# A gated linear recurrence and its two-layer MLP on one core: v cast on GpSimd, merged masks and state sums, other PSUM banks, another order of the weight loads

## The chip, the cores and the metric

One core of a Trainium2 chip runs the whole program. The metric is the device time of one execution in microseconds. Engines are named as in the profile: PE (TensorE matmul), PEld (its weight loads), DVE (VectorE), ACT (ScalarE), POOL (GpSimd), SP (SyncE, which issues every DMA here).

## The reference

Inputs r, k, v, w have the shape (4, 8, 768, 48): batch, head, position, head dimension; u is (8, 48). All are float32, and so is the output, (3072, 384).

```python
for t in range(S):
    cur = np.einsum('bhd,bhe->bhde', u[None] * kt, vt)
    y[:, :, t] = np.einsum('bhd,bhde->bhe', rt, state + cur)
    state = wt[:, :, :, None] * state + np.einsum('bhd,bhe->bhde', kt, vt)
...
h = x @ w_in                     # x: y as (3072, 384); w_in: 384 x 2048
g = np.maximum(0.01 * h, h)
return (g @ w_out)               # w_out: 2048 x 384
```

## The kernel before, in words

**Chunks.** The 768 positions of each of the 4 batches are cut into 6 chunks of 128, 24 chunks in all (NCH), and a chunk carries all 8 heads: its tiles are 128 positions x 384 columns. Within a batch the state goes from chunk to chunk. After the scan of a chunk comes its MLP.

**Scan of a chunk** (loop from line 283). Four loads bring w, k, r, v into one slot of the ring `in` (L297). ACT takes the logarithm of w (L317). PE sums it from the chunk's end with a triangular matrix and adds the totals of four head pairs (cp, L332, L337). DVE adds the logarithm again (ci, L347), ACT takes two exponentials (er L354, ek L360) and a third for the totals (a, L435), and DVE multiplies r and k with them (rk, L367, L373). PE transposes r and k, eight transposes in one step into the bank se (L385); DVE copies the r half out (rkT, L392), ACT the k half (L396). PE makes the scores, even heads in se and odd heads in so (L471); DVE masks each bank (m, two operations, L494). v is cast to bf16 on DVE (vb, L323). PE forms the chunk's sums of k times v (pp, L482). POOL scales the state with the totals, in two halves of 64 partitions (sb, L462); DVE adds pp (s, two halves, L510, or a copy in the first chunk of a batch, L508). PE adds up the output yp from rkT, sb and from m, vb (L522, L526). The u term goes by POOL and DVE: ru (L411, L415), its row sum dg (L419), times v (vs, L423). DVE adds it to yp (y, L537), PE transposes y into the bank so (L547), and ACT copies the result into xT (L553).

**MLP of a chunk.** Four up pieces (each 12 matmuls into one of two banks hp, L579), each followed by ACT's leaky ReLU (g, L613); four down quarters (each 4 matmuls into op, L631); DVE copies op (L642) and SP stores it (L646). The weights come once, four loads of 768 KB for w_in (L250) and four for w_out (L255), through slots of the same ring `in`, and DVE and ACT cast half each (L273, L275).

**What sets the order.** Every operation is a step with an engine, an assumed duration, a priority and its dependencies. The class Plan (line 16) runs a list schedule over them: the free engine takes the ready step of the lowest priority number. Each engine then executes its steps in the order that came out, whatever the real durations are. Scan steps of chunk n have the priority 10n or little more, MLP steps 1000 and up, ACT's g 5, output copies 3. `WEIGHTS` holds for each weight load the chunk ahead of whose loads it is planned, and its priority: w_in ahead of chunk 1 with 4, w_out ahead of chunk 3 with 24. The logarithm of chunk n waits for the first up piece of chunk n-4 (LEAD), the loads of chunk n for the sums cp of chunk n-5 (AHEAD). A ring of one tile makes a step wait until the readers of the tile's last use are done. PSUM has eight banks: hp two, and op, cp, se, so, yp, pp one each.

Of the kernel before, what the change touches and what calls it, by code (L numbers as in the profile page):

```python
# [8 lines left out]
F32 = mybir.dt.float32  # L9
# [6 lines left out]
class Plan:  # L16
# [3 lines left out]
    LAT = 0.12  # L20
# [15 lines left out]
    def order(self):  # L36
# [18 lines left out]
        while events:  # L55
# [14 lines left out]
            if self.wire[i] is None:  # L70
                done[i] = free[e] + self.LAT
            else:
                dma_free = max(dma_free, free[e]) + self.wire[i]
                done[i] = dma_free + 1.7
# [41 lines left out]
def kernel(  # L116
# [11 lines left out]
    nc = tc.nc  # L128
# [11 lines left out]
    APE = 24  # L140
# [4 lines left out]
    WEIGHTS = [(1, 4)] * 4 + [(3, 24)] * 4  # L145
# [22 lines left out]
    er_r = ring("er", 3, [128, H, 64], F32)  # L168
# [8 lines left out]
    a_r = ring("a", 3, [128, NP], F32)  # L177
    sx_r = ring("s", 3, [128, NP, D], F32)
# [5 lines left out]
    dram = ctx.enter_context(tc.tile_pool(name="dram", bufs=1, space=bass.MemoryType.DRAM))  # L184
    ad_r = ring("ad", 4, [1, H * 64], F32, dram)
    hp_r = ring("hp", 2, [128, 512], F32, psum)
    op_r = ring("op", 1, [128, DM], F32, psum)
    cp_r = ring("cp", 1, [128, 512], F32, psum)
    se_r = ring("se", 1, [128, NP, 128], F32, psum)
    so_r = ring("so", 1, [128, NP, 128], F32, psum)  # L190
    yp_r = ring("yp", 1, [128, H, D], F32, psum)
    pp_r = ring("pp", 1, [128, NP, 2, D], F32, psum)

    with tc.manual_schedule():
# [3 lines left out]
        for t in sb_r.tiles:  # L198
            nc.gpsimd.memset(t[:], 0.0)
        for t in er_r.tiles:  # L200
            nc.gpsimd.memset(t[:], 1.0)
# [31 lines left out]
        def dve(n, src=60):  # L233
            return (src + n) / 960.0 + 0.03

        def act(n, src=180):
            return (src + n) / 1200.0
# [7 lines left out]
        def weight_steps(q, which, pri):  # L245
# [16 lines left out]
            for half, eng in ((0, "DVE"), (1, "ACT")):  # L262
# [13 lines left out]
                d = dve(384) if eng == "DVE" else act(768, 224)  # L276
# [6 lines left out]
        for n in range(NCH):  # L283
# [19 lines left out]
            if n == 0:  # L303
# [18 lines left out]
                "DVE", dve(DM // 2),  # L322
                lambda vb=vb, vn=vn: nc.vector.tensor_copy(out=vb.t[:], in_=vn.t),  # L323
# [4 lines left out]

            a_pe = n < APE

            def cum(cp=cp, lw=lw, tot=(not first and a_pe)):
# [3 lines left out]
                if tot:  # L335
# [6 lines left out]
            s_cum = step("PE", 0.35 if not first and a_pe else 0.17, cum, P0, reads=[lw], writes=[cp], deps=[s_ln])  # L342
# [12 lines left out]
                    out=er.t[:, :, 0:D], in_=cp.t[:, 0:DM].rearrange("p (h d) -> p h d", h=H), func=AF.Exp),  # L355
                P0, reads=[cp], writes=[er], deps=[s_cum],
# [9 lines left out]
                "DVE", dve(DM),  # L366
                lambda rk=rk, rn=rn, er=er: nc.vector.tensor_tensor(  # L367
                    out=rk.t[:, 0, :, 0:D], in0=rn.t, in1=er.t[:, :, 0:D], op=ALU.mult),
# [3 lines left out]
                "DVE", dve(DM),  # L372
# [6 lines left out]
            if n < NPE:  # L379
                tr = se_r.take()  # L380
                trv = tr.t[:].bitcast(BF16).rearrange("p a (b t) -> p (a b) t", b=2)

                def tpose(rk=rk, trv=trv):
                    for g in range(2 * NP):
                        nc.tensor.transpose(  # L385
                            trv[:, g, :],
                            rk.t[:, g // NP, 2 * (g % NP) : 2 * (g % NP) + 2, :].rearrange("p h d -> p (h d)"),
                            ident[:])
                s_tr = step("PE", 0.6, tpose, P0, reads=[rk], writes=[tr], deps=[s_r, s_k])
                s_t1 = step(  # L390
                    "DVE", dve(512, 120),
                    lambda trv=trv, rkT=rkT: nc.vector.tensor_copy(out=rkT.t[:, 0:NP, :], in_=trv[:, 0:NP, :]),  # L392
                    P0, reads=[tr], writes=[rkT], deps=[s_tr])
                s_t2 = step(
                    "ACT", act(512),
                    lambda trv=trv, rkT=rkT: nc.scalar.copy(out=rkT.t[:, NP:, :], in_=trv[:, NP:, :]),  # L396
                    P0, reads=[tr], writes=[rkT], deps=[s_tr])
                s_T = [s_t1, s_t2]
            else:
                s_T = [step(  # L400
                    "SP", 0.6,
                    lambda rk=rk, rkT=rkT: nc.sync.dma_start_transpose(
                        out=rkT.t[:], in_=rk.t[:].rearrange("p a h d -> p (a h d)")),
                    P0, reads=[rk], writes=[rkT], deps=[s_r, s_k], wire=1.0)]
# [13 lines left out]
                "DVE", dve(DM),  # L418
# [3 lines left out]
                "POOL", 1.05,  # L422
# [5 lines left out]
            se, so, yp = se_r.take(), so_r.take(), yp_r.take()  # L428
            sb = None
            if not first:  # L430
                a_in = a_r.take()
                if a_pe:
                    s_adep = step(
                        "ACT", act(NP),
                        lambda a_in=a_in, cp=cp: nc.scalar.activation(  # L435
                            out=a_in.t[:], in_=cp.t[:, DM : DM + NP], func=AF.Exp),
                        P0 + 1, reads=[cp], writes=[a_in], deps=[s_cum])
                else:

                    ad = ad_r.take()  # L440
                    s_row = step(
                        "SP", 0.45,
                        lambda ad=ad, er=er: nc.sync.dma_start(
                            out=ad.t[:], in_=er.t[0:1].rearrange("o h d -> o (h d)")),
                        P0 + 1, reads=[er], writes=[ad], deps=[s_er], wire=0.02)
                    s_sp = step(
                        "SP", 0.45,
                        lambda ad=ad, a_in=a_in: nc.sync.dma_start(
                            out=a_in.t[:], in_=ad.t[:].rearrange("o (p q) -> q (o p)", p=NP)),
                        P0 + 1, reads=[ad], writes=[a_in], deps=[s_row], wire=0.4)  # L450
                    s_adep = step(
                        "DVE", dve(NP),
                        lambda a_in=a_in: nc.vector.reciprocal(out=a_in.t[:], in_=a_in.t[:]),
                        P0 + 1, reads=[a_in], deps=[s_sp])
                s_in, s_sdep = prev
                sb = sb_r.take()
                s_sb = []
                for half in range(2):
                    q0 = 64 * half
                    s_sb.append(step(  # L460
                        "POOL", 0.5,
                        lambda sb=sb, s_in=s_in, a_in=a_in, q0=q0, half=half: nc.gpsimd.tensor_tensor(  # L462
                            out=sb.t[q0 : q0 + 64, :, half, :], in0=s_in.t[q0 : q0 + 64],
                            in1=a_in.t[q0 : q0 + 64].unsqueeze(2).to_broadcast([64, NP, D]), op=ALU.mult),
                        P0 + 1, reads=[s_in, a_in], writes=[sb], deps=[*s_sdep, s_adep]))

            def scores(rkT=rkT, se=se, so=so):
                for p in range(NP):
                    for par, sc in enumerate((se, so)):
                        q0 = 64 * par  # L470
                        nc.tensor.matmul(  # L471
                            sc.t[:, p, :], lhsT=rkT.t[q0 : q0 + D, NP + p, :],
                            rhs=rkT.t[q0 : q0 + D, p, :], start=True, stop=True, skip_group_check=True)

            s_sc = step("PE", 0.42, scores, P0 + 1, reads=[rkT], writes=[se, so], deps=s_T)

            if not last:
                pp = pp_r.take()

                def sums(pp=pp, rk=rk, vb=vb):  # L480
                    for p in range(NP):
                        nc.tensor.matmul(  # L482
                            pp.t[:, p, :, :],
                            lhsT=rk.t[:, 1, 2 * p : 2 * p + 2, :].rearrange("p h d -> p (h d)"),
                            rhs=vb.t[:, 2 * p : 2 * p + 2, :],
                            start=True, stop=True, skip_group_check=True)

                s_pp = step("PE", 0.24, sums, P0 + 1, reads=[rk, vb], writes=[pp], deps=[s_k, s_vb])
            m = m_r.take()
            s_m = []  # L490
            for par, sc in enumerate((se, so)):
                s_m.append(step(
                    "DVE", dve(NP * 128, 120),
                    lambda m=m, sc=sc, par=par: nc.vector.tensor_tensor(  # L494
                        out=m.t[:, par, :, :], in0=sc.t[:],
                        in1=maskb[:].unsqueeze(1).to_broadcast([128, NP, 128]), op=ALU.mult),
                    P0 + 1, reads=[sc], writes=[m], deps=[s_sc]))


            if not last:  # L500
                sx = sx_r.take()
                s_st = []
                for half in range(2):
                    def state(half=half, sx=sx, pp=pp, sb=sb):
                        q0 = 64 * half
                        o, i = sx.t[q0 : q0 + 64], pp.t[q0 : q0 + 64, :, half, :]
                        if sb is None:
                            nc.vector.tensor_copy(out=o, in_=i)  # L508
                        else:
                            nc.vector.tensor_tensor(  # L510
                                out=o, in0=i, in1=sb.t[q0 : q0 + 64, :, half, :], op=ALU.add)

                    s_st.append(step(
                        "DVE", dve(NP * D, 120), state, P0 + 1,
                        reads=[pp] + ([] if sb is None else [sb]), writes=[sx],
                        deps=[s_pp] + ([] if sb is None else s_sb)))
                prev = (sx, s_st)

# [166 lines left out]
```

## Time and profile before

| | |
|---|---|
| median of the 2 runs | 222.24 us (221.99 and 222.48) |
| profiled execution | 222.69 us, span in the trace 220.8 us |
| busy, of the span | PE 84%, PEld 65%, DVE 70%, ACT 54%, POOL 45% |
| mean granted TensorE clock | 0.969 |
| DMA | 30.47 MB; 107179 packets, 100368 of them under 512 B |
| from an input load's issue to its landing | 4.1 to 4.4 us median; a weight load 8.2 to 8.7 |

The busy share of an engine counts the time in which it works on at least one instruction. In a table of windows each row is a stretch of the span with the busy microseconds of each engine and, in brackets, the number of its instructions; PEclk is the granted clock, DMA share the mean busy share of the 16 DMA engines. In a row of a group stand the line, engine, operation, output and inputs, then the total busy time, the mean of one in ns, and the idle time just before them with what ended it. In the waits, three figures are the total, the number of times and the longest.

### The profile page before, as it was taken

To read this page: it belongs to the slowest core of one execution; us is meant where nothing else is said; L and a number is where in the kernel's file an instruction comes from. 1 tells how busy PE (TensorE), PEld (TensorE's weight loads), DVE (VectorE), ACT (ScalarE), POOL (GpSimd) and SP (SyncE) were. 2 spreads that over 40 slices of the span, in tenths; PEclk is the share of its full clock that TensorE was granted. 3 is DMA by queue.
4 is the path that set the end of the run, shared out by engine and by line. 5 is a ranking of instruction groups with operands and counts; after the bars stand their busy time and mean duration, and the time that the engine had idled before them with its cause. 6 is when DMAs were issued, how large, how long until landed. Compare 5 with 4: busy or idle time off the path is not lost.

```text
span 220.8 us, 6043 instructions
## 1 busy us (share of the span) xinstructions
PE 186.3 (84%) x2448; PEld 144.2 (65%) x2448; DVE 155.6 (70%) x299; ACT 118.7 (54%) x245; POOL 98.6 (45%) x125
## 2 busy tenths in 40 slices
PE   0446679887979998949899999999999999999983
PEld 0246457665667776736686778777777777788861
DVE  6653995589999999996878876977967565620021
ACT  3347367565566655615465547656555655545420
POOL 6312740687663965666787573474412211200000
PEclk9999559999999999988999999999999999999999
DMA  7999999999999999939089267846010110001101
GB/s 130 318 355 184 297 355 165 179 193 189 200 185 216 188 210 201 200 76 181 18 162 177 61 122 147 174 98 128 36 39 2 37 39 36 3 36 39 39 36 71
DMA packets 107179, 30.47 MB, mean 138 GB/s; under 512 B 100368, under 2 KB 105616, under 8 KB 107152
## 3 DMA queue, kind: packets, MB, share of 16 engines
q1 hardware_dynamic: 107152, 30.09, 64.7%
q8 instruction: 19, 0.31, 0.6%
q14 instruction: 8, 0.07, 0.1%
HBM read 25.36 MB, written 4.72 MB: 136 GB/s over the span
## 4 chain that ended last, share of the span: by engine, by line
PE 49%; DVE 23%; DMA 8%; ACT 7%; issue 7%; SPq 2%; POOL 2%; DVEq 0%; ACTq 0%; POOLq 0%
PE hp L579 19%; PE op L631 18%; DVE rk L373 4%; DVE ci L347 3%; DMA in<-in_moe_w_in_dram 3%; DVE m L494 3%; PE se L385 3%; DVE s L510 3%; PE se L471 3%; DMA in<-in_w_dram 2%; DVE y L537 2%; ACT er L354 2%; DMA in<-in_r_dram 2%; DVE vb L323 2%; PE so L547 2%
## 5 line engine op out<-in xcount | busy, mean ns | idle before, releaser
L579 PE MATMUL hp<-xT,w_in_b 128*128 128x128 bf16 x1152 | 81.0, 225 | 0.8 <-ACT xT L553 0.8
L613 ACT ACTIVATE g<-hp 128x512 bf16<-128x512 f32 x96 | 57.4, 598 | 39.4 <-PE hp L579 38.5
L631 PE MATMUL op<-w_out_b,g 128*128 128x384 bf16 x384 | 77.8, 329 | 0.6 <-DVE o L642 0.6
L579 PEld LDWEIGHTS <-w_in_b 128*128 128x128 bf16 x1152 | 72.5, 101 | 7.5 <-issue 1.2
L631 PEld LDWEIGHTS <-g 128*128 128x128 bf16 x384 | 33.1, 98 | 16.5 <-issue 1.8
L462 POOL TENSOR_TENSOR sb<-s,a 64x192 bf16<-64x192 f32 x40 | 25.6, 639 | 28.8 <-ACT a L435 24.9
L411 POOL TENSOR_TENSOR ru<-in,ub 128x384 f32<-128x384 f32 x24 | 24.7, 1033 | 25.0 <-DMA in<-in_r_dram 21.1
L423 POOL TENSOR_TENSOR vs<-in,dg 128x384 f32<-128x384 f32 x24 | 20.0, 834 | 35.2 <-DVE dg L419 11.4
L642 DVE COPY o<-op 128x384 f32<-128x384 f32 x24 | 13.3, 555 | 23.2 <-PE op L631 22.8
L415 POOL TENSOR_TENSOR ru<-ru,in 128x384 f32<-128x384 f32 x24 | 25.7, 1074 | 1.5
L385 PE MATMUL se<-ident,rk 128*128 128x128 bf16 x192 | 18.3, 230 | 7.8 <-DVE rk L367 3.9
L396 ACT COPY rkT<-se 128x512 bf16<-128x512 bf16 x24 | 14.0, 585 | 19.2 <-DVE rkT L392 12.8
L494 DVE TENSOR_TENSOR m<-se,maskb 128x512 bf16<-128x512 f32 x24 | 16.5, 689 | 6.8 <-ACT g L613 3.7
L385 PEld LDWEIGHTS <-rk 128*128 128x128 bf16 x192 | 12.5, 101 | 12.7 <-DVE rk L373 6.0
L367 DVE TENSOR_TENSOR rk<-in,er 128x384 bf16<-128x384 f32 x24 | 18.2, 759 | 2.3 <-ACT er L354 2.1
L347 DVE TENSOR_TENSOR ci<-cp,lw 128x384 f32<-128x384 f32 x24 | 13.3, 553 | 8.3 <-PE cp L337 5.1
L373 DVE TENSOR_TENSOR rk<-in,ek 128x384 bf16<-128x384 f32 x24 | 18.0, 750 | 1.2 <-ACT ek L360 1.1
L537 DVE TENSOR_TENSOR y<-yp,vs 128x384 bf16<-128x384 f32 x24 | 13.2, 550 | 7.8 <-PE yp L526 7.7
L354 ACT ACTIVATE er<-cp 128x384 f32<-128x384 f32 x24 | 11.8, 491 | 10.6 <-DVE ci L347 6.1
L547 PE MATMUL so<-ident,y 128*128 128x128 bf16 x72 | 8.5, 231 | 9.5 <-DVE y L537 9.2
L494 DVE TENSOR_TENSOR m<-so,maskb 128x512 bf16<-128x512 f32 x24 | 16.3, 680 | 0.0
L360 ACT ACTIVATE ek<-ci 128x384 f32<-128x384 f32 x24 | 12.5, 520 | 5.8 <-DVE ci L347 5.8
(42 smaller groups left out, 193.1 us busy)
## 6 DMA issues: line engine op xcount, KB each, us to landing
in<-in_w_dram SPq DMA_DIRECT2D x24, 192.0 KB, 4.2
in<-in_k_dram SPq DMA_DIRECT2D x24, 192.0 KB, 4.1
in<-in_r_dram SPq DMA_DIRECT2D x24, 192.0 KB, 4.4
in<-in_v_dram SPq DMA_DIRECT2D x24, 192.0 KB, 4.4
out_dram<-o SPq DMA_DIRECT2D x24, 192.0 KB, 2.0
in<-in_moe_w_in_dram SPq DMA_DIRECT2D x4, 768.0 KB, 8.2
in<-in_moe_w_out_dram SPq DMA_DIRECT2D x4, 768.0 KB, 8.7
ub<-in_u_dram SPq DMA_DIRECT2D x1, 192.0 KB, 5.0
```

The source lines that it names most:

```text
L347: lambda cp=cp, ci=ci, lw=lw: nc.vector.tensor_tensor(out=ci.t[:], in0=cp.t[:, 0:DM].rearrange("p (h d) -> p h d", h=H), in1=lw.t[:, :, 0: ...
L367: lambda rk=rk, rn=rn, er=er: nc.vector.tensor_tensor(out=rk.t[:, 0, :, 0:D], in0=rn.t, in1=er.t[:, :, 0:D], op=ALU.mult),
L373: lambda rk=rk, kn=kn, ek=ek: nc.vector.tensor_tensor(out=rk.t[:, 1, :, 0:D], in0=kn.t, in1=ek.t[:], op=ALU.mult),
L385: nc.tensor.transpose(trv[:, g, :], rk.t[:, g // NP, 2 * (g % NP) : 2 * (g % NP) + 2, :].rearrange("p h d -> p (h d)"), ident[:])
L411: lambda ru=ru, rn=rn: nc.gpsimd.tensor_tensor(out=ru.t[:], in0=rn.t, in1=ubv, op=ALU.mult),
L415: lambda ru=ru, kn=kn: nc.gpsimd.tensor_tensor(out=ru.t[:], in0=ru.t[:], in1=kn.t, op=ALU.mult),
L423: lambda vs=vs, vn=vn, dg=dg: nc.gpsimd.tensor_tensor(out=vs.t[:], in0=vn.t, in1=dg.t[:].unsqueeze(2).to_broadcast([128, H, D]), op=ALU.mult),
L462: lambda sb=sb, s_in=s_in, a_in=a_in, q0=q0, half=half: nc.gpsimd.tensor_tensor(out=sb.t[q0 : q0 + 64, :, half, :], in0=s_in.t[q0 : q0 + 6 ...
L494: lambda m=m, sc=sc, par=par: nc.vector.tensor_tensor(out=m.t[:, par, :, :], in0=sc.t[:], in1=maskb[:].unsqueeze(1).to_broadcast([128, NP, ...
L579: nc.tensor.matmul(hp.t[:, a * N : (a + 1) * N], lhsT=w_in_b[:, t, (j + a) * 128 : (j + a + 1) * 128], rhs=xT[:, t, c0 : c0 + N], start=(a ...
L613: lambda hp=hp, g=g, j=j, J=J, N=N: nc.scalar.activation(out=g.t[:, j : j + J, 0:N], in_=hp.t[:, 0 : J * N].rearrange("p (a n) -> p a n", ...
L631: nc.tensor.matmul(op.t[:], lhsT=g.t[:, j, off : off + 128], rhs=w_out_b[:, j, :], start=(j == 0), stop=(j == NJ - 1))
```

## The change

- The v cast goes from DVE to POOL. Both masks are one DVE operation of 1024 columns over a tile `sc` of two banks. The state has both heads of a pair side by side, so sb is one POOL operation and s one DVE operation of 384 columns; the totals' exponential is two ACT operations of 64 partitions each, into a tile that is zero elsewhere.
- The transposes of r and of k are two steps of four, each in its bank of `sc`, each with its copy. The scores use the same tile afterwards.
- pp, yp and the transposes of y share one bank, `yp`. The output op has two banks.
- w_in is requested ahead of chunk 2 with priority 14, w_out ahead of chunk 4 with 34.
- The planner's latencies and many assumed durations are other numbers. A branch that was not used (totals by way of DRAM) is gone.

```diff
-    LAT = 0.12
+    LAT = {"PE": 0.28, "DVE": 0.07, "ACT": 0.07, "POOL": 0.07, "SP": 0.07}
...
-    WEIGHTS = [(1, 4)] * 4 + [(3, 24)] * 4
+    WEIGHTS = [(2, 14)] * 4 + [(4, 34)] * 4
...
-    op_r = ring("op", 1, [128, DM], F32, psum)
+    op_r = ring("op", 2, [128, DM], F32, psum)
     cp_r = ring("cp", 1, [128, 512], F32, psum)
-    se_r = ring("se", 1, [128, NP, 128], F32, psum)
-    so_r = ring("so", 1, [128, NP, 128], F32, psum)
-    yp_r = ring("yp", 1, [128, H, D], F32, psum)
-    pp_r = ring("pp", 1, [128, NP, 2, D], F32, psum)
+    yp_r = pp_r = ring("yp", 1, [128, 512], F32, psum)
+    sc_r = ring("sc", 1, [128, 2, NP, 128], F32, psum)
...
             s_vb = step(
-                "DVE", dve(DM // 2),
-                lambda vb=vb, vn=vn: nc.vector.tensor_copy(out=vb.t[:], in_=vn.t),
+                "POOL", 0.8,
+                lambda vb=vb, vn=vn: nc.gpsimd.tensor_copy(out=vb.t[:], in_=vn.t),
                 P0 + 2, reads=[vn], writes=[vb], deps=[vl],
...
+                for a, s_d, eng in ((0, s_r, "DVE"), (1, s_k, "ACT")):
+                    def tpose(rk=rk, trv=trv, a=a):
+                        for g in range(NP):
+                            nc.tensor.transpose(
+                                trv[:, a, g, :],
+                                rk.t[:, a, 2 * g : 2 * g + 2, :].rearrange("p h d -> p (h d)"),
+                                ident[:])
...
+                    s_tr = step("PE", 0.23, tpose, P0, reads=[rk], writes=[tr], deps=[s_d])
...
+                for half in range(2):
+                    q0 = 64 * half
+                    s_adep.append(step(
+                        "ACT", 0.17,
+                        lambda a_in=a_in, cp=cp, q0=q0, half=half: nc.scalar.activation(
+                            out=a_in.t[q0 : q0 + 64, :, half], in_=cp.t[q0 : q0 + 64, DM : DM + NP], func=AF.Exp),
...
+                s_sb = [step(
+                    "POOL", 1.05,
+                    lambda sb=sb, s_in=s_in, a_in=a_in: nc.gpsimd.tensor_tensor(
+                        out=sb.t[:].rearrange("p g a d -> p (g a) d"),
+                        in0=s_in.t[:].rearrange("p g a d -> p (g a) d"),
+                        in1=a_in.t[:].rearrange("p g a -> p (g a)").unsqueeze(2).to_broadcast([128, H, D]),
...
+            s_m = [step(
+                "DVE", 1.2,
+                lambda m=m, sc=sc: nc.vector.tensor_tensor(
+                    out=m.t[:].rearrange("p a g t -> p (a g) t"),
+                    in0=sc.t[:].rearrange("p a g t -> p (a g) t"),
+                    in1=maskb[:].unsqueeze(1).to_broadcast([128, H, 128]), op=ALU.mult),
...
+                        nc.vector.tensor_tensor(out=sx.t[:], in0=pp.t[:, 0:DM].rearrange("p (g a d) -> p g a d", g=NP, a=2), in1=sb.t[:], op=ALU.add)
...
-                tr = so_r.take()
-                trv = tr.t[:].bitcast(BF16).rearrange("p a (b t) -> p (a b) t", b=2)
+                trv = yp.t[:].bitcast(BF16).rearrange("p (g t) -> p g t", t=128)
```

The change moves instructions on every engine. On SP, at the start, before (in_69 holds chunk 0, in_70 to in_73 w_in, in_74 chunk 1):

```order
L306 DMA ub<-in_u_dram 128x384
L250 DMA in_70<-in_moe_w_in_dram 128x3x512
L250 DMA in_71<-in_moe_w_in_dram 128x3x512
L250 DMA in_72<-in_moe_w_in_dram 128x3x512
L250 DMA in_73<-in_moe_w_in_dram 128x3x512
L297 DMA in_74<-in_w_dram 128x8x48
L297 DMA in_74<-in_k_dram 128x8x48
L297 DMA in_74<-in_r_dram 128x8x48
L297 DMA in_74<-in_v_dram 128x8x48
```
And in the change (in_70 is chunk 1 now, in_71 to in_74 are w_in):

```order
L299 DMA ub<-in_u_dram 128x384
L290 DMA in_70<-in_w_dram 128x8x48
L290 DMA in_70<-in_k_dram 128x8x48
L290 DMA in_70<-in_r_dram 128x8x48
L290 DMA in_70<-in_v_dram 128x8x48
L243 DMA in_71<-in_moe_w_in_dram 128x3x512
L243 DMA in_72<-in_moe_w_in_dram 128x3x512
L243 DMA in_73<-in_moe_w_in_dram 128x3x512
L243 DMA in_74<-in_moe_w_in_dram 128x3x512
```
Chunk 1's inputs have moved ahead of w_in.

Further down the same queue, before: w_out into in_76 to in_79, then the loads of chunk 4 (in_70) and chunk 3 (in_69, which chunk 0 had held):

```order
L255 DMA in_76<-in_moe_w_out_dram 128x4x384
L255 DMA in_77<-in_moe_w_out_dram 128x4x384
L255 DMA in_78<-in_moe_w_out_dram 128x4x384
L255 DMA in_79<-in_moe_w_out_dram 128x4x384
L297 DMA in_70<-in_w_dram 128x8x48
L297 DMA in_70<-in_k_dram 128x8x48
L297 DMA in_69<-in_w_dram 128x8x48
L297 DMA in_69<-in_k_dram 128x8x48
L297 DMA in_69<-in_r_dram 128x8x48
L297 DMA in_69<-in_v_dram 128x8x48
L297 DMA in_70<-in_r_dram 128x8x48
L297 DMA in_70<-in_v_dram 128x8x48
```
And in the change, where chunk 3 has the fresh slot in_76 and chunk 4 has in_70:

```order
L290 DMA in_76<-in_w_dram 128x8x48
L290 DMA in_76<-in_k_dram 128x8x48
L290 DMA in_76<-in_r_dram 128x8x48
L290 DMA in_76<-in_v_dram 128x8x48
L248 DMA in_77<-in_moe_w_out_dram 128x4x384
L248 DMA in_78<-in_moe_w_out_dram 128x4x384
L248 DMA in_79<-in_moe_w_out_dram 128x4x384
L248 DMA in_69<-in_moe_w_out_dram 128x4x384
L290 DMA in_70<-in_w_dram 128x8x48
L290 DMA in_70<-in_k_dram 128x8x48
```
Chunk 3 stands ahead of w_out now, and chunk 4 behind it.

On DVE, from the r multiply of chunk 9 (in_75) to that of chunk 10 (in_76), before; rows of other chunks stand between them:

```order
L367 TENSOR_TENSOR rk_91<-in_75,er_85 128x8x48
L494 TENSOR_TENSOR m_115<-se_147,maskb 128x512
L494 TENSOR_TENSOR m_115<-so_148,maskb 128x512
L373 TENSOR_TENSOR rk_91<-in_75,ek_89 128x8x48
L323 CAST vb_101<-in_75 128x384
L419 TENSOR_REDUCE dg_106<-ru_105 128x8
L347 TENSOR_TENSOR ci_83<-cp_146,lw_81 128x384
L537 TENSOR_TENSOR y_125<-yp_149,vs_109 128x384
L392 COPY rkT_95<-se_147 128x512
L510 TENSOR_TENSOR s_121<-pp_150,sb_123 64x192 x2
L367 TENSOR_TENSOR rk_92<-in_76,er_86 128x8x48
```
And in the change:

```order
L360 TENSOR_TENSOR rk_91<-in_75,er_85 128x8x48
L366 TENSOR_TENSOR rk_91<-in_75,ek_89 128x8x48
L616 COPY o_134<-op_140 128x384
L512 TENSOR_TENSOR y_125<-yp_142,vs_109 128x384
L387 COPY rkT_95<-sc_143 128x512
L340 TENSOR_TENSOR ci_83<-cp_141,lw_81 128x384
L414 TENSOR_REDUCE dg_108<-ru_105 128x8
L471 TENSOR_TENSOR m_113<-sc_143,maskb 128x1024
L485 TENSOR_TENSOR s_121<-yp_142,sb_123 128x384
L360 TENSOR_TENSOR rk_92<-in_76,er_86 128x8x48
```
Between the two multiplies of r the cast is gone, mask and state sum are one row each, and y comes before the mask.

More of the change, by code (lines that the diff above doesn't have):

```diff
@@ L139 @@
     NQ = FF // 512
-    APE = 24
     NPE = 24
@@ L197 @@
             nc.vector.memset(t[:], 0.0)
-        for t in sb_r.tiles:
+        for t in a_r.tiles:
             nc.gpsimd.memset(t[:], 0.0)
-        for t in er_r.tiles:
-            nc.gpsimd.memset(t[:], 1.0)
         nc.vector.memset(ones[:], 1.0)
@@ L340, in cum @@
                             rhs=ones[:], start=True, stop=True, skip_group_check=True)
-            s_cum = step("PE", 0.35 if not first and a_pe else 0.17, cum, P0, reads=[lw], writes=[cp], deps=[s_ln])
+            s_cum = step("PE", 0.27 if not first else 0.165, cum, P0, reads=[lw], writes=[cp], deps=[s_ln])
             cums.append(s_cum)
@@ L431 @@
                 a_in = a_r.take()
[L432 to L454, printed above, removed]
@@ L456 @@
                 sb = sb_r.take()
[L457 to L465, printed above, removed]
@@ L502, with state @@
                 s_st = []
[L503 to L516, printed above, removed]
+                def state(sx=sx, pp=pp, sb=sb):
+                    if sb is None:
+                        nc.vector.tensor_copy(out=sx.t[:], in_=pp.t[:, 0:DM].rearrange("p (g a d) -> p g a d", g=NP, a=2))
+                    else:
+                        nc.vector.tensor_tensor(out=sx.t[:], in0=pp.t[:, 0:DM].rearrange("p (g a d) -> p g a d", g=NP, a=2), in1=sb.t[:], op=ALU.add)
+                s_st.append(step(
+                    "DVE", 0.55, state, P0 + 1, reads=[pp] + ([] if sb is None else [sb]), writes=[sx],
+                    deps=[s_pp] + ([] if sb is None else s_sb)))
                 prev = (sx, s_st)
+            yp = yp_r.take()
             def intra(m=m, vb=vb, yp=yp, rkT=rkT, sb=sb):
```

112 lines of the change are left out of this document (50 added, 62 removed).

## The prediction

> **What bounds the kernel now.** I read the page first, then the table of windows, then the waits and the timeline of the early part.
>
> ```profile
> span 220.8 us, 6043 instructions
> PE 186.3 (84%) x2448; PEld 144.2 (65%) x2448; DVE 155.6 (70%) x299; ACT 118.7 (54%) x245; POOL 98.6 (45%) x125
> ```
> No engine is full over the span, so the shares must be cut into stretches.
>
> ```profile
> core 0: us, PE busy (x) PEld busy (x) DVE busy (x) ACT busy (x) POOL busy (x), PEclk, DMA share, GB/s
> 0.00:40.00 40.00, 23.36 (x246) 18.20 (x247) 25.60 (x53) 20.82 (x37) 14.74 (x26) 0.87 1.00 254
> 40.00:100.00 60.00, 50.73 (x703) 38.81 (x702) 56.57 (x103) 33.23 (x74) 41.02 (x48) 0.98 1.04 185
> 100.00:160.00 60.00, 56.97 (x793) 44.37 (x790) 48.00 (x95) 35.59 (x76) 37.00 (x43) 0.99 0.60 119
> 160.00:200.00 40.00, 38.45 (x539) 30.38 (x537) 23.22 (x45) 22.99 (x49) 5.81 (x9) 1.00 0.08 30
> ...
> ```
> There are three regimes. Up to 40 us the DMA engines are full (share 1.00) and PE is idle for 16.6 us. From 40 to 100 us DVE is full (56.57 of 60) and PE is idle for 9.3. From 100 us PE is the bound (3.0 idle in 60, then 1.6 in 40), and DVE has room.
>
> The same windows for the two MLP lines, L579 first and L631 second, count what PE got done:
>
> ```profile
> 0.00:40.00 40.00, 10.10 (x114) 9.56 (x115) 0.87 1.00 254
> 40.00:100.00 60.00, 20.07 (x286) 17.32 (x283) 0.98 1.04 185
> 100.00:160.00 60.00, 24.99 (x369) 22.31 (x370) 0.99 0.60 119
> ```
> ```profile
> 0.00:40.00 40.00, 4.61 (x20) 1.92 (x20) 0.87 1.00 254
> 40.00:100.00 60.00, 18.39 (x92) 7.82 (x92) 0.98 1.04 185
> 100.00:160.00 60.00, 25.66 (x124) 10.49 (x124) 0.99 0.60 119
> ```
> Busy time counts pipelined matmuls too long; what one costs in a full queue is read from the chain near the end, where nothing else runs:
>
> ```profile
> 204.10 1.34 PE hp L579 x24
> 205.44 0.65 PE op L631 x4
> ```
> That is 0.056 us per up matmul and 0.1625 per down matmul, so 48 and 16 of them make 5.3 us of MLP per chunk. In 100 to 160 us the MLP took 369 x 0.056 + 124 x 0.1625 = 40.8 us; with 3.0 idle, 16.2 are left for some 8.5 chunks of scan, 1.9 us each. PE's whole work is thus 24 x (5.3 + 1.9) = 173 us of 220.8. The other 48 are what a change can reach. In 40 to 100 us the MLP took only 286 x 0.056 + 92 x 0.1625 = 31.0 us.
>
> **Term 1, the order of the loads.** The timeline shows what the old order does to chunk 3, and how fast transfers go:
>
> ```profile
> 8.65 0.99 POOL L411 TENSOR_TENSOR ru<-in,ub 128x384 f32<-128x384 f32 x1 [3.74 <-DMA ub<-in_u_dram]
> ...
> 10.48 0.83 ACT L275 CAST w_in_b<-in 128x768 bf16<-128x768 f32 x1 [1.51 <-DMA in<-in_moe_w_in_dram]
> ...
> 14.52 0.69 DVE L273 CAST w_in_b<-in 128x768 bf16<-128x768 f32 x1 [0.88 <-DMA in<-in_moe_w_in_dram]
> ...
> 40.34 1.00 POOL L411 TENSOR_TENSOR ru<-in,ub 128x384 f32<-128x384 f32 x1 [8.43 <-DMA in<-in_r_dram]
> ...
> 43.46 0.94 SPq L297 DMA_DIRECT2D in<-in_w_dram  x1
> 44.45 0.94 SPq L297 DMA_DIRECT2D in<-in_k_dram  x1
> ```
> A weight quarter lands every 2 us (first and third waited for, 10.5 and 14.5), an input load every 0.98 us when the queue is full, u by 8.6. Chunk 3's r, requested behind w_out and two loads of chunk 4, lands only at 40.3. In the new order I get: chunk 1 at about 12.5 (8.6 + 4 x 0.98), w_in at 14.5 to 21, chunk 2 at 25, chunk 3 at 28.7, w_out at 31 to 37, chunk 4 at 41. The sum of bytes is the same, so nothing after chunk 4 comes earlier. What is late now: w_in by 4 us and w_out by about as much as one chunk's loads. PE's new order has both first up layers before 24 us, three scans by 30, and then down quarters, each as its weights arrive; behind the first stand chunk 2's y transposes, and ACT's copy and chunk 3 wait for those. By 40 us I count 11.5 up pieces (7.7 us), 6.5 down quarters (4.2 us) and four scans (7.4 us), 19.3 us of work. Before had 114 x 0.056 + 20 x 0.1625 = 9.6 us of MLP and three scans (5.7 us), 15.3. **Gain 4.0 us**; bounds are -2 (PE stands at the first down quarter until all of w_out is there) and 7 (the clock, 0.87 on the mean in this stretch, holds up better because PE idles less).
>
> **Term 2, DVE between 40 and 100 us.** Groups by form (busy, mean ns):
>
> ```profile
> L415 POOL TENSOR_TENSOR ru<-ru,in 128x384 f32<-128x384 f32 x24 | 25.7, 1074 | 1.5
> L462 POOL TENSOR_TENSOR sb<-s,a 64x192 bf16<-64x192 f32 x40 | 25.6, 639 | 28.8 <-ACT a L435 24.9 <-ACT er L354 1.5 <-DVE s L510 0.6
> L411 POOL TENSOR_TENSOR ru<-in,ub 128x384 f32<-128x384 f32 x24 | 24.7, 1033 | 25.0 <-DMA in<-in_r_dram 21.1 <-DMA ub<-in_u_dram 3.7
> L423 POOL TENSOR_TENSOR vs<-in,dg 128x384 f32<-128x384 f32 x24 | 20.0, 834 | 35.2 <-DVE dg L419 11.4 <-DVE y L537 9.0 <-PE cp L337 5.5
> ...
> L494 DVE TENSOR_TENSOR m<-se,maskb 128x512 bf16<-128x512 f32 x24 | 16.5, 689 | 6.8 <-ACT g L613 3.7 <-PE so L471 2.5 <-issue 0.2
> ...
> L323 DVE CAST vb<-in 128x384 bf16<-128x384 f32 x24 | 14.4, 607 | 0.0
> ...
> L537 DVE TENSOR_TENSOR y<-yp,vs 128x384 bf16<-128x384 f32 x24 | 13.2, 550 | 7.8 <-PE yp L526 7.7
> ...
> L553 ACT COPY xT<-so 128x384 bf16<-128x384 bf16 x24 | 11.4, 476 | 7.4 <-PE so L547 7.4
> L510 DVE TENSOR_TENSOR s<-pp,sb 64x192 f32<-64x192 f32 x32 | 11.2, 350 | 0.6
> ...
> L199 POOL MEMSET sb<- 128x384 bf16 x3 | 1.1, 417 | 0.3 <-POOLq L669 0.3
> ```
> DVE loses the v cast, 0.61 us a chunk. One mask of 1024 columns in place of two of 512 saves at least nothing and at most the fixed part of one, 0.689 - 512/960 = 0.16; I take 0.16. One state sum of 384 columns is nearest to y (same size, one PSUM and one SBUF input), 0.55 for 2 x 0.35: 0.15. That is 0.92 a chunk, some 9 chunks in this stretch, with the cast at its cost here:
>
> ```profile
> 40.00:100.00 60.00, 9.60 (x13) 0.98 1.04 185
> ```
> (the cast's own row, 0.74 us each). 9.6 + 9 x 0.31 = 12.4 us leave DVE, and its 56.57 become 44, or 46 with longer waits at the shared port (below). That is the 48.00 of the next window, where PE idles 3.0. So I let PE work in this stretch as in the next: 40.8 - 31.0 = 9.8 us more MLP, less one scan that the early stretch has more (1.9): **gain 8 us**. Bounds: 0, if DVE or the port still sets the pace, and 10, if PE hardly idles.
>
> **The new load of POOL.** The cast there is between the memset of the same output (0.42) and the two-input L411 (1.03); I take 0.8, by L423. sb as one operation has L423's form and size, 0.83 to 1.03 in place of 2 x 0.64. POOL goes from 1.03 + 1.07 + 0.83 + 1.28 = 4.2 to about 4.6 us a chunk, and the idle time that L462 and L423 show covers it; if that is gone, a late vb holds up pp on PE.
>
> **Term 3, waits that go and come.** The waits in order of size:
>
> ```profile
> ACT rkT L396 <- DVE rkT L392: 12.8, 17, 1.8
> ...
> PE so L547 <- DVE y L537: 9.2, 8, 2.6
> ```
> The two copies of the transposes ran one after the other, ACT behind DVE; with a bank each they can run together, about 0.4 us a chunk off the scan's chain. Two waits grow. The next transposes wait for the whole mask, 1.2 us, where the first half, 0.69, was enough. And sums, output and y transposes share one bank: pp of a chunk waits for ACT's copy of the chunk before, and PE's queue behind it, mostly MLP, waits too. I take the three as even, bounds 0.5 us a chunk either way. The second exponential on ACT (0.17 us) is covered by ACT's 46% idle, else it costs 0.17 on the way to sb. The output's second bank takes one wait from the end:
>
> ```profile
> 214.64 2.76 PE L631 MATMUL op<-w_out_b,g 128*128 128x384 bf16 x16 [0.65 <-DVE o L642]
> ```
> **Gain 0.6.** Between 100 and 200 us, of 4.6 idle, I take 1.0. POOL's memsets shrink at the start, but PE's first matmul waits for a DVE memset chain that stays: nothing.
>
> **Sum.** 4.0 + 8.0 + 0.6 + 1.0 = 13.6. The profiled execution took 222.69 around its span of 220.8, and the median of the runs shown is 0.45 lower, 222.24. So 222.24 - 13.6 = 208.6, and I forecast **209.5 us**, one us kept back for the port.
>
> **Rivals.** *The port takes the gain of term 2.* The rows and what they show:
>
> ```profile
> L367 DVE TENSOR_TENSOR rk<-in,er x24: 541/636/1386, 6.2 to 188.8; 128x384 bf16<-128x384 f32 x24
> 27.12 0.99 POOL L411 TENSOR_TENSOR ru<-in,ub 128x384 f32<-128x384 f32 x1
> 27.14 1.39 DVE L367 TENSOR_TENSOR rk<-in,er 128x384 bf16<-128x384 f32 x1
> ```
> The DVE multiply that starts behind a POOL operation takes 1.39 us for 0.54: it waits until POOL is done. Each chunk has two such multiplies, and five POOL operations to wait for. If every multiply waits 0.4 more, 0.8 a chunk, DVE keeps its old pace: 222.24 - 4.0 - 0.6 = 217.6. For it: POOL is at 41 of 60 already, and grows. Against: the cast itself leaves the port's customers on DVE, and 4.6 + 2 x 0.54 = 5.7 us of port time fit in 7.2 of PE. The Trainium skill states this rule outright (SBUF — State Buffer, "Who interferes with whom": a GpSimd operation and a DVE one with two SBUF inputs exclude each other for a whole instruction), and the pair of rows agrees.
>
> *The down weights come late.* Term 1 at its lower bound of -2: 222.24 + 2 - 9.6 = 214.6. For it: eight input loads now stand ahead of w_out. Against: the DMA engines are full in either order.
>
> *One bank for sums, output and transposes stalls PE.* Two rows of the chain of waits give what PE has in it:
>
> ```profile
> 52.08 0.34 PE so L547 x3
> 52.42 0.17 PE pp L482 x4
> ```
> With pp 0.17, s 0.55, yp about 0.4 (an estimate: its twelve matmuls against the four of pp), y 0.55, transposes 0.34 and xT 0.48 the chain is 2.5 us, and each of six handovers can stand behind one operation of 0.6: 6.1. With two more it passes PE's 7.2, and PE stands at pp. From 0.6 us a chunk (13.6 over 23) it eats all gains; at 0.85 the time is 208.6 + 19.5 = **228**, slower. For it: the waits for y above are of this kind and reach 2.6 us. Against: y's transposes waited on the scores' bank in the same way.
>
> **How the numbers follow.** Forecast 0.62, with its own range 201 to 216; port 0.17; late weights 0.11; bank 0.10. A measurement tells about 2% from no change, 217.8 to 226.7. Faster: nearly all of the forecast, half of the port, most of the late weights, 0.76. Within: 0.15. Slower: 0.09, the bank. The range 201 to 220 leaves out the bank, the port's upper part and 3% below.
>
> **What would show it.** Right: chunk 3's inputs land before 30 us; PE idles under 4 us between 40 and 100; DVE there is under 50 of 60; no wait of 0.65 at the end. Wrong: DVE at 55 or more there with multiplies of 0.9 us and over (port); PE waiting for ACT's xT at the sums (bank); PE idle past 35 us at the first down quarter (weights).

## The result and the profile after

The change took 205.64 us (205.64 and 205.65), before 222.24: ratio 0.925, interval 0.921 to 0.930. The forecast was 209.5 us, range 201 to 220. The time fits; what follows shows that the reason given for the largest term does not.

The page, and the table of windows (columns as before):

```profile
span 203.9 us, 6000 instructions
...
PE 179.8 (88%) x2448; PEld 141.5 (69%) x2448; DVE 140.6 (69%) x231; ACT 120.7 (59%) x265; POOL 102.4 (50%) x126
```
```profile
0.00:40.00 40.00, 23.20 (x270) 17.57 (x271) 28.70 (x50) 21.94 (x43) 18.05 (x29) 0.91 0.99 252
40.00:100.00 60.00, 58.40 (x832) 46.07 (x828) 49.42 (x82) 39.84 (x93) 48.15 (x56) 1.00 1.10 197
100.00:160.00 60.00, 58.41 (x847) 46.78 (x846) 47.70 (x77) 38.86 (x90) 33.69 (x39) 1.00 0.55 115
```
PE idles for 1.6 us between 40 and 100, where it idled for 9.3, and for 16.8 up to 40 (16.6 before). The same windows for the up matmuls (L553) and the down matmuls (L605):

```profile
0.00:40.00 40.00, 8.61 (x120) 7.83 (x120) 0.91 0.99 252
40.00:100.00 60.00, 25.14 (x363) 21.53 (x360) 1.00 1.10 197
100.00:160.00 60.00, 26.79 (x386) 23.40 (x387) 1.00 0.55 115
```
```profile
0.00:40.00 40.00, 3.79 (x13) 1.57 (x14) 0.91 0.99 252
40.00:100.00 60.00, 26.02 (x132) 11.24 (x131) 1.00 1.10 197
100.00:160.00 60.00, 26.30 (x130) 10.76 (x128) 1.00 0.55 115
```
At 0.056 and 0.1625 us a matmul this is 8.8 us of MLP up to 40 us (before 9.6), 41.8 between 40 and 100 (31.0), and 42.7 from 100 to 160 (40.8). Most of the gain lies between 40 and 100 us.

The groups of the changed operations:

```profile
L471 DVE TENSOR_TENSOR m<-sc,maskb 128x1024 bf16<-128x1024 f32 x24 | 29.3, 1220 | 11.4 <-PE sc L450 9.9 <-ACT lw L310 1.3 <-ACT ek L353 0.2
...
L418 POOL TENSOR_TENSOR vs<-in,dg 128x384 f32<-128x384 f32 x24 | 22.3, 931 | 17.1 <-DVE y L512 12.1 <-DVE dg L414 5.0
L366 DVE TENSOR_TENSOR rk<-in,ek 128x384 bf16<-128x384 f32 x24 | 21.8, 907 | 0.0
...
L439 POOL TENSOR_TENSOR sb<-s,a 128x384 bf16<-128x384 f32 x20 | 18.5, 924 | 25.3 <-ACT a L432 23.4 <-DVE s L485 1.6
L360 DVE TENSOR_TENSOR rk<-in,er 128x384 bf16<-128x384 f32 x24 | 18.3, 765 | 3.4 <-ACT er L347 2.3 <-DMA in<-in_r_dram 0.7
...
L316 POOL CAST vb<-in 128x384 bf16<-128x384 f32 x24 | 12.9, 536 | 10.5 <-DMA in<-in_v_dram 8.6 <-PE hp L553 1.8
...
L485 DVE TENSOR_TENSOR s<-yp,sb 128x384 f32<-128x384 f32 x16 | 8.8, 552 | 3.4 <-PE yp L461 3.0 <-POOL vs L418 0.3
```
Mask 1.22 and state sum 0.55 are what was forecast; the cast costs POOL 0.54 (forecast 0.8), sb 0.92. The multiply of k grew from 0.75 to 0.91, that of r stayed.

The last row of down matmuls on the timeline runs through without the wait of 0.65 us:

```profile
196.58 3.41 PE L605 MATMUL op<-w_out_b,g 128*128 128x384 bf16 x20
```

### The profile page after: what moved, and what is told of

It is laid out like the page before. It is cut to its first block, busy times and chain, and to the rows that moved or that the text cites. A ratio compares the mean times of both kernels' runs of the same rounds, so it can differ in the third digit from the quotient of the medians.

```text
span 203.9 us, 6000 instructions
## 1 busy us (share of the span) xinstructions
PE 179.8 (88%) x2448; PEld 141.5 (69%) x2448; DVE 140.6 (69%) x231; ACT 120.7 (59%) x265; POOL 102.4 (50%) x126
## 4 chain that ended last, share of the span: by engine, by line
PE 68%; DVE 11%; ACT 6%; DMA 5%; POOL 3%; issue 2%; SPq 1%; DVEq 0%
PE op L605 26%; PE hp L553 25%; PE sc L379 5%; PE sc L450 3%; DVE rk L366 2%; DMA in<-in_r_dram 2%; DMA in<-in_w_dram 2%; PE yp L501 2%; DVE m L471 2%; PE cp L325 2%; DVE rkT L387 2%; DVE rk L360 2%; ACT g L587 2%; PE yp L461 1%; PE yp L521 1%
## 5 line engine op out<-in xcount | busy, mean ns | idle before, releaser
L553 PE MATMUL hp<-xT,w_in_b 128*128 128x128 bf16 x1152 | 80.4, 220 | 1.3 <-ACT xT L527 0.9
L605 PE MATMUL op<-w_out_b,g 128*128 128x384 bf16 x384 | 78.2, 330 | 0.0
L553 PEld LDWEIGHTS <-w_in_b 128*128 128x128 bf16 x1152 | 70.5, 99 | 9.0 <-issue 1.0
L605 PEld LDWEIGHTS <-g 128*128 128x128 bf16 x384 | 33.3, 98 | 14.2 <-issue 0.7
L471 DVE TENSOR_TENSOR m<-sc,maskb 128x1024 bf16<-128x1024 f32 x24 | 29.3, 1220 | 11.4 <-PE sc L450 9.9
L439 POOL TENSOR_TENSOR sb<-s,a 128x384 bf16<-128x384 f32 x20 | 18.5, 924 | 25.3 <-ACT a L432 23.4
L418 POOL TENSOR_TENSOR vs<-in,dg 128x384 f32<-128x384 f32 x24 | 22.3, 931 | 17.1 <-DVE y L512 12.1
L379 PE MATMUL sc<-ident,rk 128*128 128x128 bf16 x192 | 19.2, 230 | 5.6 <-DVE rk L360 3.2
L389 ACT COPY rkT<-sc 128x512 bf16<-128x512 bf16 x24 | 14.1, 586 | 14.5 <-PE sc L379 7.1
L366 DVE TENSOR_TENSOR rk<-in,ek 128x384 bf16<-128x384 f32 x24 | 21.8, 907 | 0.0
L316 POOL CAST vb<-in 128x384 bf16<-128x384 f32 x24 | 12.9, 536 | 10.5 <-DMA in<-in_v_dram 8.6
L414 DVE TENSOR_REDUCE dg<-ru 128x8 f32<-128x384 f32 x24 | 13.1, 545 | 6.4 <-POOL ru L410 6.3
L310 ACT ACTIVATE lw<-in 128x384 bf16<-128x384 f32 x24 | 12.6, 523 | 2.5 <-DMA in<-in_w_dram 2.4
```

Source lines behind the costliest of these rows:

```text
L366: lambda rk=rk, kn=kn, ek=ek: nc.vector.tensor_tensor(out=rk.t[:, 1, :, 0:D], in0=kn.t, in1=ek.t[:], op=ALU.mult),
L379: nc.tensor.transpose(trv[:, a, g, :], rk.t[:, a, 2 * g : 2 * g + 2, :].rearrange("p h d -> p (h d)"), ident[:])
L389: nc.scalar.copy(out=o, in_=i)
L418: lambda vs=vs, vn=vn, dg=dg: nc.gpsimd.tensor_tensor(out=vs.t[:], in0=vn.t, in1=dg.t[:].unsqueeze(2).to_broadcast([128, H, D]), op=ALU.mult),
L439: lambda sb=sb, s_in=s_in, a_in=a_in: nc.gpsimd.tensor_tensor(out=sb.t[:].rearrange("p g a d -> p (g a) d"), in0=s_in.t[:].rearrange("p g ...
L471: lambda m=m, sc=sc: nc.vector.tensor_tensor(out=m.t[:].rearrange("p a g t -> p (a g) t"), in0=sc.t[:].rearrange("p a g t -> p (a g) t"), ...
```

## The experiments

A first theory is the prediction's: DVE was full between 40 and 100 us, and its relief is the gain (load; theory one in the expectations). The rival: the planner's new numbers put the steps into an order that fits their real durations (order; theory two). All ratios are to the kernel before, run beside them on the same chip. It took 225.0 to 226.4 us there, and 222.24 in the runs that the prediction and the expectations start from; an expected time is therefore held against ratio x 222.24.

**One edit alone, on the kernel before.** First the cast:

```diff
-                "DVE", dve(DM // 2),
-                lambda vb=vb, vn=vn: nc.vector.tensor_copy(out=vb.t[:], in_=vn.t),
+                "POOL", 0.8,
+                lambda vb=vb, vn=vn: nc.gpsimd.tensor_copy(out=vb.t[:], in_=vn.t),
```


> The kernel before with one edit: v is cast on POOL (planned at 0.8 us), all else as it was. If DVE's load between 40 and 100 us was the bound (theory one), this edit alone frees 9.6 of the 56.6 busy us there, and most of the gain of that stretch comes: 212 to 216 us. If the planner's numbers were the cause (theory two: steps stood in the wrong order for their real durations), the old numbers keep the stalls: 219 to 222 us.

219.4 us, ratio 0.973 (0.966 to 0.979): by that scale 216 us, a third of the gain. That is the upper edge of what the first theory expected and less than the rival's 219 to 222, so this run alone does not decide against the load. The window 40 to 100 us, all engines, then the up and the down matmuls (L579, L631):

```profile
40.00:100.00 60.00, 55.20 (x770) 42.38 (x769) 50.44 (x95) 36.37 (x80) 49.62 (x64) 0.99 1.04 190
```
```profile
40.00:100.00 60.00, 22.85 (x330) 19.95 (x329) 0.99 1.04 190
```
```profile
40.00:100.00 60.00, 21.97 (x108) 9.22 (x108) 0.99 1.04 190
```
DVE has as much room as in the change (50.4 against 49.4 of 60), yet PE gets 36.0 us of MLP: 5.0 more than before, and not the 10.8 more of the change. Up to 40 us the same edit lost MLP work: 75 up and 8 down matmuls, 5.5 us for 9.6. Moving one operation also gave the planner another order, so this run holds both effects.

Then the planner's numbers, with every operation left where it was:

```diff
-    LAT = 0.12
+    LAT = {"PE": 0.28, "DVE": 0.07, "ACT": 0.07, "POOL": 0.07, "SP": 0.07}
...
-            return (src + n) / 960.0 + 0.03
+            return (src + n) / 960.0 + 0.05
...
-                "DVE", dve(DM // 2),
+                "DVE", 0.6,
...
-                s_tr = step("PE", 0.6, tpose, P0, reads=[rk], writes=[tr], deps=[s_r, s_k])
+                s_tr = step("PE", 0.46, tpose, P0, reads=[rk], writes=[tr], deps=[s_r, s_k])
...
-                "PE", 0.45 if sb is None else 0.68, intra, P0 + 1,
+                "PE", 0.21 if sb is None else 0.38, intra, P0 + 1,
```


> The kernel before with the planner's new numbers alone: the change's latencies and durations, and for operations that the change no longer has their measured means (cast 0.6, eight transposes 0.46 us). No work leaves an engine. Theory one (load): DVE stays full between 40 and 100 us, 219 to 223 us. Theory two (order): at least half of the 16.6 us, 214 us or less, with fewer waits on PE between 40 and 100.

206.8 us, ratio 0.918 (0.911 to 0.925): the whole gain. The same three rows:

```profile
40.00:100.00 60.00, 58.29 (x839) 46.69 (x837) 52.22 (x103) 40.16 (x87) 37.81 (x46) 1.00 1.05 194
```
```profile
40.00:100.00 60.00, 25.48 (x380) 22.61 (x381) 1.00 1.05 194
```
```profile
40.00:100.00 60.00, 25.06 (x124) 10.51 (x124) 1.00 1.05 194
```
DVE executes 103 operations in this window, as many as in the kernel before, and is less busy (52.2 against 56.6); the MLP gets 41.4 us. The number of DVE's operations was not the bound.

Then the loads:

```diff
-    WEIGHTS = [(1, 4)] * 4 + [(3, 24)] * 4
+    WEIGHTS = [(2, 14)] * 4 + [(4, 34)] * 4
```


> The kernel before with the new order of the weight loads alone. The prediction gave the loads 4 us: 218 us. The change's own trace shows by 40 us only 120 up and 13 down matmuls against 114 and 20, so that the loads bring one scan more and no MLP: 220 to 222 us. A rival: with the scan further ahead, DVE's backlog between 40 and 100 us is smaller and the gain shows there, 215 us or less.

219.2 us, ratio 0.974 (0.968 to 0.980), by the scale 216.4: between the prediction's 4 us and the rival. By 40 us it had 120 up and 6 down matmuls, 7.7 us of MLP, no more than the change.

**One part undone, on the changed kernel.** The cast back on DVE:

```diff
-                "POOL", 0.8,
-                lambda vb=vb, vn=vn: nc.gpsimd.tensor_copy(out=vb.t[:], in_=vn.t),
+                "DVE", 0.6,
+                lambda vb=vb, vn=vn: nc.vector.tensor_copy(out=vb.t[:], in_=vn.t),
```


> The changed kernel with the v cast back on DVE, planned at 0.6 us. Theory one: DVE gets some 8 us back between 40 and 100, where it is busy 49.4 of 60, and is full again: 211 to 214 us. Theory two: the planner knows the cost and places it well: 205 to 208 us. Either way the multiplies of r and k get shorter than 0.77 and 0.91 us, since one POOL operation fewer holds the port.

205.2 us, ratio 0.911 (0.905 to 0.916), by the scale 202.4: nothing is lost. The multiplies, expected to be shorter, are so only for k:

```profile
L366 DVE TENSOR_TENSOR rk<-in,ek 128x384 bf16<-128x384 f32 x24 | 19.8, 824 | 0.0
L360 DVE TENSOR_TENSOR rk<-in,er 128x384 bf16<-128x384 f32 x24 | 19.4, 809 | 1.7 <-ACT er L347 0.9 <-DMA in<-in_r_dram 0.8
```
The mask and the state sum in two operations each:

```diff
-            s_m = [step(
-                "DVE", 1.2,
-                lambda m=m, sc=sc: nc.vector.tensor_tensor(
+            s_m = [step(
+                "DVE", 0.69,
+                lambda m=m, sc=sc, a=a: nc.vector.tensor_tensor(
+                    out=m.t[:, a], in0=sc.t[:, a],
+                    in1=maskb[:].unsqueeze(1).to_broadcast([128, NP, 128]), op=ALU.mult),
+                P0 + 1, reads=[sc], writes=[m], deps=[s_sc]) for a in range(2)]
...
+                for half in range(2):
+                    def state(sx=sx, pp=pp, sb=sb, q0=64 * half):
```


> The changed kernel with the mask and the state sum in two operations each again, on the new banks (the state sum's halves are 64 partitions of 384 columns, 0.55 us each, so this costs DVE more than the old halves did). Mask 2 x 0.69 for 1.22, state 1.10 for 0.55: 0.7 us a chunk more on DVE. If DVE is still close to its bound between 40 and 100 us (49.4 of 60), 6 us more work there cost 1 to 4 us: 207 to 210. If PE alone bounds, 206 us.

205.7 us, ratio 0.911 (0.903 to 0.920): nothing is lost either, and PE idles for 0.3 us between 40 and 100, with DVE at 51.9:

```profile
40.00:100.00 60.00, 59.66 (x798) 46.47 (x797) 51.93 (x90) 38.24 (x87) 43.64 (x51) 0.97 1.00 194
```
The old order of the loads:

```diff
-    WEIGHTS = [(2, 14)] * 4 + [(4, 34)] * 4
+    WEIGHTS = [(1, 4)] * 4 + [(3, 24)] * 4
```


> The changed kernel with the old order of the weight loads (w_in ahead of chunk 1, w_out ahead of chunk 3). By the prediction's first term it loses 4 us: 209.6 us. By the trace of the change (one scan more by 40 us, no more MLP) it loses 1 to 2: 206.6 to 207.6 us. If the loads and the relief of DVE only work together (the backlog of the scan is what DVE has to work off between 40 and 100 us), it loses 5 or more: 211 us and above.

209.2 us, ratio 0.925 (0.919 to 0.931), by the scale 205.6: no loss beside the change's first measurement, 0.5% beside its second (below). The planner's old numbers:

```diff
-    LAT = {"PE": 0.28, "DVE": 0.07, "ACT": 0.07, "POOL": 0.07, "SP": 0.07}
+    LAT = dict.fromkeys(("PE", "DVE", "ACT", "POOL", "SP"), 0.12)
...
-                "DVE", 0.7,
+                "DVE", dve(DM),
...
-                "PE", 0.21 if sb is None else 0.38, intra, P0 + 1,
+                "PE", 0.45 if sb is None else 0.68, intra, P0 + 1,
```


> The changed kernel with the planner's old numbers (latency 0.12 everywhere, multiplies at 0.49, PE steps too long; mask and state sum at twice the old halves). No work moves between engines. Theory one (load): 205.6 to 208 us. Theory two (order): 212 us or more, with PE waiting for DVE between 40 and 100 us.

217.8 us, ratio 0.965 (0.956 to 0.973), by the scale 214.4: the only part whose loss is large. Between 40 and 100 us DVE is at 49.7, the MLP at 316 x 0.056 + 110 x 0.1625 = 35.6:

```profile
40.00:100.00 60.00, 53.16 (x746) 41.23 (x744) 49.66 (x77) 36.59 (x85) 43.93 (x52) 1.00 1.04 195
```
The rest of the change, with the old numbers, is still 3.5% faster than the kernel before. Whether by its shorter work or by the other order that it brings is not separated; beside the new numbers it adds nothing (below, where the change is run once more).

**Which of the numbers.** Three parts of the second experiment, each alone on the kernel before, and the change once more beside them:

```diff
-                s_up = step("PE", J * 3 * max(N / 2400 + 0.003, 0.06), lambda up=up, hp=hp: up(hp), pri,
+                s_up = step("PE", J * 3 * (N / 2400 + 0.0025), lambda up=up, hp=hp: up(hp), pri,
```


> The kernel before with the planner's new PE durations alone (up piece 0.67 for 0.72, eight transposes 0.46 for 0.6, output matmuls 0.38 for 0.68, and the like); PE's steps of one chunk are planned at 7.2 us in place of 8.0. New theory (pace): the old plan thinks that PE is slower than it is, so PE reaches the scan's steps before their inputs are there and stands; then this edit alone brings half or more of what all new numbers bring together (0.918): 0.96 or less. Rival (the other engines' durations): 0.98 or more.

Ratio 0.959 (0.952 to 0.967), 216.0 us.

```diff
-                "DVE", dve(DM),
+                "DVE", 0.7,
```


> The kernel before with the new durations of DVE, ACT and POOL alone (multiplies 0.7 for 0.49, cast 0.6 for 0.29, copy of the transposes 0.42 for 0.69, sums 0.54 for 0.49, and the like). Rival theory (multiplies and cast are planned too short, so that PE's queue holds steps that wait for DVE): half or more of the gain of all new numbers, 0.96 or less. By the theory of PE's pace: 0.98 or more.

Ratio 0.947 (0.939 to 0.954), 213.5 us. Its window 40 to 100 us, all engines:

```profile
40.00:100.00 60.00, 58.17 (x828) 45.60 (x825) 55.22 (x108) 38.95 (x85) 39.88 (x47) 1.00 0.98 185
```
DVE is nearly as busy as in the kernel before (55.2 against 56.6), and yet PE idles for only 1.8 us and the MLP gets 348 x 0.056 + 124 x 0.1625 = 39.6.

```diff
-    LAT = 0.12
+    LAT = {"PE": 0.28, "DVE": 0.07, "ACT": 0.07, "POOL": 0.07, "SP": 0.07}
...
-                done[i] = dma_free + 1.7
+                done[i] = dma_free + 1.5
```


> The kernel before with the planner's new latencies alone: 0.28 us behind a PE step and 0.07 behind one of another engine, for 0.12 everywhere, and 1.5 for 1.7 us behind a transfer. By the theory of PE's pace, and by that of DVE's durations: 0.98 to 1.00. If the handover behind PE is what the old plan had wrong: 0.96 or less.

Ratio 0.973 (0.965 to 0.981), 219.4 us. PE's durations bring half of the gain and the other engines' a little more; neither theory of a single wrong number stands. Their gains do not add (4.1, 5.3 and 2.7 against 8.2% together).

> The changed kernel itself once more, beside the three others on one chip, so that its ratio can be set against theirs and against 0.918 of the new numbers alone and 0.911 of the change with the cast on DVE. If moving the cast and merging bring anything, it stands below those: 0.91 or less. If only the planner's numbers count, it stands at 0.91 to 0.925.

Ratio 0.920 (0.914 to 0.927), 207.4 us: beside 0.918 of the numbers alone the change shows no more. In this profile of the same kernel PE idles for 3.9 us between 40 and 100 and the MLP gets 346 x 0.056 + 124 x 0.1625 = 39.5; by so much two profiles of one kernel can differ there.

Three single edits had gained 2.6 to 2.7% each, so that the old order could merely have been an unlucky one. The last run moved PE's numbers the other way:

```diff
-                s_up = step("PE", J * 3 * max(N / 2400 + 0.003, 0.06), lambda up=up, hp=hp: up(hp), pri,
+                s_up = step("PE", J * 3 * 0.0642, lambda up=up, hp=hp: up(hp), pri,
...
-                "PE", 0.45 if sb is None else 0.68, intra, P0 + 1,
+                "PE", 0.69 if sb is None else 0.98, intra, P0 + 1,
```


> The kernel before with the planner's PE durations moved by the same steps the other way, further from what the trace measures (up piece 0.77, eight transposes 0.74, output matmuls 0.98 us, and so on). If numbers that fit the trace make the order better, this is no faster than before: ratio 1.00 or more. If the order of the kernel before is only an unlucky one, and any other order gains about as much as three of the single edits did (0.973 each), this gains too: 0.95 to 0.98.

234.7 us, ratio 1.043 (1.035 to 1.051). Not every other order gains: for PE's numbers the direction counted. It is one order only, and no other set of wrong numbers was run. Window 40 to 100 us, all engines:

```profile
40.00:100.00 60.00, 48.44 (x668) 36.53 (x665) 54.10 (x101) 32.67 (x73) 44.86 (x51) 0.99 1.01 176
```
Again DVE looks nearly full, on 101 operations, while PE idles for 11.6 us.

## Why the prediction was right in its size and wrong in its reason

**The step that failed** is the reading of the second regime: "From 40 to 100 us DVE is full (56.57 of 60)", so that 12.4 us less work on DVE would let PE run as it does later. The numbers alone give the same 41 us of MLP there with every DVE operation in place; the cast alone gives DVE the same room and brings 5.0 of the 10.8 us; the cast and the merges can be undone at no loss; and DVE at 55.2 of 60 left PE only 1.8 us of idle time (the other engines' durations alone). What the runs show in its place is the order: the planner's numbers alone bring ratio 0.918. How the old order held PE up is read from the waits: DVE worked through its queue in an order that was late for PE, with operations stretched beside POOL. In the kernel before, three casts stand in DVE's queue ahead of the y for which PE waits:

```profile
94.34 3.28 DVE L323 CAST vb<-in 128x384 bf16<-128x384 f32 x3
97.55 0.55 DVE L537 TENSOR_TENSOR y<-yp,vs 128x384 bf16<-128x384 f32 x1
```
```profile
98.15 0.50 PE L547 MATMUL so<-ident,y 128*128 128x128 bf16 x3 [2.62 <-DVE y L537]
```
POOL meanwhile runs without a pause:

```profile
93.01 2.26 POOL L411 TENSOR_TENSOR ru<-in,ub 128x384 f32<-128x384 f32 x2
95.24 2.17 POOL L415 TENSOR_TENSOR ru<-ru,in 128x384 f32<-128x384 f32 x2
```
Each cast was planned at 0.29 us and took 1.1, the length of a POOL operation beside it; for PE the plan had 8.0 us a chunk in place of 7.2. So PE came to the scan's steps early, DVE to its own late, and PE's whole queue stood. This is the longest wait of its kind; that the others came about in the same way is argued from it, not shown. With the new numbers (the second experiment) the casts stand apart, one a chunk:

```profile
61.68 0.67 DVE L494 TENSOR_TENSOR m<-so,maskb 128x512 bf16<-128x512 f32 x1
62.28 0.34 DVE L323 CAST vb<-in 128x384 bf16<-128x384 f32 x1
...
68.11 0.56 DVE L537 TENSOR_TENSOR y<-yp,vs 128x384 bf16<-128x384 f32 x1 [0.17 <-PE yp L526]
68.58 0.35 DVE L323 CAST vb<-in 128x384 bf16<-128x384 f32 x1
```
The largest of PE's waits from 40 to 200 us, before and then with the numbers alone (total, times, longest):

```profile
PE so L547 <- DVE y L537: 5.3, 6, 2.6
PE se L385 <- DVE rk L373: 2.9, 6, 1.0
PE se L471 <- DVE s L510: 1.8, 6, 0.3
```
```profile
PE op L631 <- DVE o L642: 0.9, 2, 0.6
PE so L547 <- DVE y L537: 0.7, 1, 0.7
```
That the change moves the order on every engine was stated; that the planner's numbers are an edit with a price of its own was not, and no rival held it.

**Term 1**, 4.0 us for the loads, was too large. The arrivals came about as worked out:

```profile
25.00 1.00 POOL L406 TENSOR_TENSOR ru<-in,ub 128x384 f32<-128x384 f32 x1 [7.48 <-DMA in<-in_r_dram]
...
29.67 0.50 POOL L316 CAST vb<-in 128x384 bf16<-128x384 f32 x1
```
Chunk 2 was there at 25.0, chunk 3 before 30. But chunk 2's scan took longer than the 5 us that were left for it:

```profile
32.74 0.50 PE L501 MATMUL yp<-vb,m 128*128 128x48 bf16 x8 [1.90 <-DVE m L471]
33.07 1.21 PE L379 MATMUL sc<-ident,rk 128*128 128x128 bf16 x8
34.13 1.44 PE L605 MATMUL op<-w_out_b,g 128*128 128x384 bf16 x4
```
Its output stands behind the mask until 32.7, and the first down quarter follows at 34.1; by 40 us there were 13 down matmuls, where the prediction counted 6.5 quarters, 26. By then PE had done 0.8 us less MLP than before and, of a fourth scan, the transposes, scores and sums but not the output. At the planner's new durations these are 1.3 us, an estimate that leaves a gain of about half a us. In the changed kernel, the loads undone show no loss that can be told from nothing (0.925, against 0.920 and 0.925 for the change itself). In the kernel before, the same edit brought 2.6%; there it also gave the planner another order, and the two effects are not separated.

**Term 3.** The bank for sums, output and transposes was no bound: no wait of PE's sums for xT is among the waits, and PE idles for 1.6 us in 60. The second output bank took the 0.65 us from the end. **The port** took 0.16 us a chunk from the multiply of k, not 0.8: that rival fell, though the pair of rows behind it was read rightly. From 100 to 160 us the MLP gained 1.9 us, and the outputs of one more scan fell into that window (9 for 8), where 1.0 was forecast up to 200.

**The signs that were named** came true (inputs of chunk 3 before 30 us, PE's idle time under 4, DVE under 50, no wait at the end), and they come true under the other theory as well. They could tell that the time would come, not why.

That the sum came within 4 us of the time is in part luck: term 1 was some 3.5 us too large, the stretch from 40 to 100 us brought 10.8 us of MLP where 8 were forecast, and by another cause, and the window from 100 to 160 us brought 1.9 of MLP where 1.0 was forecast up to 200.

What stays open: which of the two halves, PE's durations or the others', would matter in which order, since their gains overlap; and whether the change without the cast's move is really 1% faster than with it (0.911, 0.905 to 0.916, against 0.920, 0.914 to 0.927, and 0.925, 0.921 to 0.930: the first two intervals overlap). It is the fastest kernel measured here, with the one that splits the masks. Open too is how much of the gain of the new order comes from fewer DVE operations stretched beside POOL, and how much from PE's steps standing where their inputs are ready.

## What to carry to other kernels

An engine that is busy 94% of a stretch is not thereby shown to be the bound where queues run in a fixed order: compare how much of the waiting engine's work is done per operation of the busy one, and try another order with the same work first. Where a planner sets the order, its assumed durations are part of the kernel; take them from the profile, stretched operations included, before moving work between engines. Numbers that were off by at most about 0.3 us a step cost this kernel 8%, and PE's alone, moved as far again, another 4%.

## What the runs showed of the hardware

The cast of v takes POOL 0.50 us when nothing stretches it (0.54 on the mean), half of a POOL operation with two inputs (1.0), and DVE 0.35 at best and up to 1.15 beside POOL. The granted clock was 0.62 between 31 and 40 us of the changed kernel, while PE was busy for 7.3 of those 9 us; the wait of 1.90 us shown above lies in this stretch, and whether it set the clock is not shown:

```profile
31.00:40.00 9.00, 7.26 (x68) 4.90 (x69) 8.00 (x12) 4.74 (x8) 3.17 (x4) 0.62 1.04 321
```
